# Zero matmuls in TensorE's early gaps, and a new planned order, in a fused decay-attention and feed-forward kernel

## The chip, the cores and the metric

The kernel runs on one core of a Trainium2 chip. The metric is the device time of one launch in microseconds; the median over several runs is compared. The core has five engines with their own instruction queues: TensorE (PE) for matmuls, VectorE (DVE), ScalarE (ACT), GpSimd (POOL), and SyncE (SP), which here issues all DMAs. TensorE writes its results to PSUM, and in this kernel only VectorE and ScalarE read them there.

## The reference

Inputs are q, k, v and f_logit, each of shape (4, 8, 768, 48): 4 batches, 8 heads, 768 steps, 48 channels; and two weights, w_in (384 x 2048) and w_out (2048 x 384). All are float32, and so is the output (3072, 384).

```python
f = 1.0 / (1.0 + np.exp(-f_logit))
for t in range(S):
    state = f[:, :, t, :, None] * state + np.einsum('bhd,bhe->bhde', k[:, :, t], v[:, :, t])
    y[:, :, t] = np.einsum('bhd,bhde->bhe', q[:, :, t], state)
x = y.transpose(0, 2, 1, 3).reshape(B * S, H * D)
h = x @ w_in
out = (h * np.cos(h)) @ w_out
```

So the first part is a gated linear attention whose state decays per channel, and the second a feed-forward layer with h cos(h) as its activation.

## The kernel before

**Tiles.** The 768 steps of a batch are cut into six chunks of 128 steps, which gives 24 chunks n = 0 to 23. For each chunk the cumulated log decay is a matmul with a triangular matrix (L505 to L517), two exponentials give b and bi (L522), and q times b and k times bi are the bf16 pair qk (L567, L680). TensorE transposes qk (L587, L698), or from chunk 12 on mostly a DMA does (L689). Then come the scores (L600, L711), their mask (am, L606, L714), the chunk's contribution to the state (L620, L724), which VectorE and GpSimd add and decay into sz (L540, L547), and the output y, already transposed (L653, L744). Its copy is xT (L458). Chunks 0 to 11 are worked on in pairs (DUAL: 0, 2, 4, 6, 8, 10), whose loads hold two consecutive steps per row.

**The feed-forward part** works on 13 units of tokens: two of 128 and eleven of 256 (`UNITS`). For each unit, `h` (L768) multiplies xT by w_in into two banks of PSUM, ScalarE takes the cosine (L775), VectorE the product gT (L778), and `o` (L790) multiplies gT by w_out. ot is the copy that SyncE stores (L799, L802). A unit's `h` is split into parts j, each of which reads its own columns of w_in and depends on no other part. Both weights are loaded in four blocks each (L424), through the buffers of gT, and cast to bf16 by one of three engines (L430).

**Groups.** Four chunks make a group of the decay; its exponentials and logarithm need another table on ScalarE than the cosine, so each group locks that table until it is done. From the second group on, the first `exp` waits for all the group's loads of f, and a "gate" makes it wait for a given number of cosines (`PR["gate"]`).

**What sets the order.** No engine's order follows the loops. `build` lists some 800 operations with a cost for each engine that can take them, the values that they read and write, and a priority from the table `PR`. `Plan.run` then simulates the engines: of the operations that can start on an engine within 120 ns of the earliest one, it takes the one with the lowest priority number, gives it a buffer, and moves that engine's clock on. `PIN` binds single operations, by number, to one engine. The instructions are then emitted in the order of planned starts. So a load is issued when its buffer is free and its priority is the lowest among those left; transfers follow one another on a planned bus. The planner knows of a slow clock of TensorE: a value `hot` rises with busy time and falls with idle time, both with a constant of 2500 ns, and below 0.5 a matmul group costs 1.9 times as much.

**PSUM** has eight banks, held as four tiles of two. `apart` tells the dependency tracking that two operations on different banks of one tile do not conflict.

Of the kernel before, what the change touches and what calls it, by code (L numbers as in the profile page):

```python
# [10 lines left out]
BF16 = mybir.dt.bfloat16  # L11
# [105 lines left out]
class Plan:  # L117
# [4 lines left out]
    FORM = 96.0  # L122
    TABLE = 1290.0
# [34 lines left out]
    def run(self):  # L158
        free = {"PE": 0.0, "ACT": 800.0, "DVE": 3500.0, "POOL": 4500.0, "SP": 750.0}
        table, lock, bus, hot, pe_end, form, sent = None, None, 0.0, 0.0, 0.0, "full", []  # L160
        left = {}
# [7 lines left out]
        order, n = [], len(self.ops)  # L169
        while len(order) < n:  # L170
# [46 lines left out]
            o.cost = cost  # L217
            if e == "PE":
                hot *= math.exp((pe_end - s) / 2500.0)
                if hot < 0.5:  # L220
                    cost *= 1.9
                hot = 1.0 - (1.0 - hot) * math.exp(-cost / 2500.0)
                pe_end, form = s + cost, o.form[1]
            o.start = s
            free[e] = s + cost
            if o.dma is not None:
                bus = max(s + cost + 700.0, bus) + o.dma
                o.end = bus + 1250.0
                sent.append(bus)
                if len(sent) > 3:  # L230
                    free[e] = max(free[e], sent[-4] + 900.0)
            else:
                o.end = s + cost + (self.PE_LAT if e == "PE" else 55.0 if e in ("ACT", "DVE") else 0.0)
                o.lat = o.end - s - cost
# [13 lines left out]
        order.sort(key=lambda o: (o.start, o.seq))  # L248
        self.makespan = max(o.end for o in order)
# [3 lines left out]
def apart(tc, o, base):  # L253
# [13 lines left out]
    if banks and len(others) == len(banks):  # L267
        for b in banks:
# [11 lines left out]
    "at": [1.29, -46.96, -60.77, -65.31, -72.81, -88.9, -62.2, -78.56, -65.41, -84.16, -49.49, 6.81, 12.89,  # L280
          14.83, 48.99, 87.93, 101.11, 142.54, 101.56, 112.3, 125.58, 54.78, 57.75, 54.86],
    "dec": [47.91, 7.43, -56.35, -90.55, -146.08, -64.43],
    "f": [-34.92, 30.83, -12.01, 57.34, 6.81, 46.82, 6.06, 8.26, 16.01, 51.17, 25.08, -28.88, 70.17, 25.27,
          33.52, 29.11, 45.05, 53.82, 30, 41.02, 75.42, 105.25, 101.8, 47.02],
    "h": [18.15, -30.97, -41.55, -0.98, 22.93, -34.89, 0.62, 10.73, 30.17, 30.71, 68.39, 4.86, 95.08],
    "k": [-26.25, -35.58, -7.84, -14.12, 9.23, 20.62, 9.36, 29.64, 15.73, -3.08, 14.9, 28.23, 13.74, 17.17,
          50.2, 52.92, 39.09, 29.41, 58.65, 34.81, 116.3, 77.26, 139.17, 143.04],
    "o": [24.63, -19.31, 41.7, 78.77, 63.07, 110.4, 28.5, 147.24, 133.25, 171.17, 181.78, 182.53, 223.04],
    "tq": [40.18, 24.86, 49.05, 16.89, -14.63, -13.53, -72.99, 30.71, 100.53, 84.21, 40.41, 92.28, 63.29,
          8.72, -34.92, -31.89, -4.13, 9.55, 29.5, 39.68, 64.12, 95.56, 100.49, 121.09],  # L290
    "v": [-13.48, 17.98, -0.36, -1.26, 5.93, -16.14, 10.21, 31.08, 11.8, 9.11, 19.3, 20.54, 41.94, 22.2,
          47.4, 31.46, 38.38, 19.76, 32.92, 47.16, 53.68, 101.87, 117.21, 44.48],
    "w_in": [-6.83, -2.34, 0.21, 1.62],
    "w_out": [4.81, 3.28, 2.34, 8.4],
    "wc": [-90.87, -90.11, -69.83, -52.76, -136.89, -232, -120.5, -196.66],
    "gate": [None, 8, 6, 1, 19, 12],
}
PIN = {1: "POOL", 3: "ACT", 5: "ACT", 9: "DVE", 11: "POOL", 13: "DVE", 34: "POOL", 37: "POOL", 39: "ACT", 43:
       "ACT", 54: "DVE", 55: "DVE", 82: "DVE", 102: "POOL", 103: "POOL", 104: "DVE", 105: "POOL", 107: "DVE",
       111: "DVE", 124: "ACT", 164: "DVE", 165: "POOL", 167: "ACT", 169: "ACT", 182: "DVE", 204: "DVE", 210:  # L300
       "ACT", 222: "DVE", 228: "DVE", 243: "ACT", 244: "ACT", 283: "POOL", 284: "POOL", 286: "DVE", 293: "ACT",
       306: "ACT", 333: "DVE", 346: "POOL", 347: "POOL", 348: "POOL", 349: "POOL", 364: "ACT", 386: "ACT", 415:
       "ACT", 430: "ACT", 451: "DVE", 457: "DVE", 472: "POOL", 481: "ACT", 487: "ACT", 496: "DVE", 517: "DVE",
       523: "ACT", 547: "DVE", 558: "ACT", 579: "DVE", 585: "DVE", 600: "POOL", 608: "DVE", 623: "ACT", 644:
       "DVE", 665: "POOL", 674: "DVE", 680: "ACT", 689: "DVE", 731: "ACT", 740: "DVE", 746: "ACT", 752: "DVE",
       773: "DVE", 779: "ACT"}


def build(nc, cpool, ppool, q, k, v, f_logit, moe_w_in, moe_w_out, out):
# [11 lines left out]
    def tl(shape, dt, name):  # L321
        return cpool.tile(shape, dt, name=name)

    ident = tl([128, 128], BF16, "ident")
# [70 lines left out]
    P.banks = base  # L395
    HB = lambda a, d=D: a.rearrange("p (h d) -> p h d", d=d)
# [36 lines left out]
    def load(t, src, b, c, n, prio, nm, flat=lambda a: a):  # L433

        if n not in DUAL:
            P.op(nm + str(n), {"SP": 430.0}, lambda e: nc.sync.dma_start(
                out=HB(t.ap), in_=src[b, :, c * C:(c + 1) * C, :].rearrange("h p d -> p h d")),
                writes=[t], prio=prio, dma=1050.0)
            return
# [235 lines left out]
    def attend(b, c, n, ld, bt, bi, i, prio):  # L675
# [12 lines left out]
        if n in TURN_QK:  # L688
            P.op("tq", {"SP": 420.0}, lambda e: nc.sync.dma_start_transpose(out=qkt.ap, in_=qk.ap),  # L689
                 reads=[qk], writes=[qkt], prio=PR["tq"][n], dma=1600.0)  # L690
# [64 lines left out]
    def moe(t0, T):  # L755
# [26 lines left out]
        for i in range(T // C):  # L782
            r0, ot, pr = t0 + i * C, Val(otS), PR["o"][UNIT[t0]] + i
            pieces = [(0, d_model)] if r0 + C < n_tokens else [(0, 256), (256, d_model)]
            for a, z in pieces:
# [10 lines left out]
                def store(e, half=half, r0=r0, a=a, z=z):  # L796
# [4 lines left out]
                    else:  # L801
                        nc.sync.dma_start(out=out[r0:r0 + C, a:z], in_=half.ap)  # L802
                P.op("st_o", {"SP": 420.0 if r0 // C // 2 * 2 not in DUAL else 840.0}, store, reads=[half],
                     prio=pr, dma=545.0 * (z - a) / d_model)
# [33 lines left out]
def kernel(  # L838
# [13 lines left out]
    with tc.manual_schedule():  # L852
# [4 lines left out]
        for o in order:  # L857
# [4 lines left out]
            del made[:]  # L862
            o.fn(o.eng)
# [33 lines left out]
```

## Time and profile before

| | |
|---|---|
| median of 5 runs | 191.67 us (190.46 to 192.27) |
| the profiled execution | 192.27 us, its span from first to last instruction 190.5 us |
| TensorE busy | 178.1 us (94%) |
| VectorE, ScalarE, GpSimd busy | 131.1, 125.8, 68.1 us |
| moved by DMA | 33.14 MB, 174 GB/s over the span |

The profile is of one execution. In a row of groups, "x24" is a count; a bracket tells the engine's idle time before the group and what ended it. The 40 slices are of 4.76 us each; a digit is a busy share in tenths. "PEclk" is the clock that the throttle granted. Matmuls are pipelined, so the duration of one matmul is longer than the distance between two; the time of a group over its count is nearer to the cost.

### The profile page before, as it was taken

To read this page: it belongs to the slowest core of one execution; us is meant where nothing else is said; L and a number is where in the kernel's file an instruction comes from. 1 tells how busy PE (TensorE), PEld (TensorE's weight loads), DVE (VectorE), ACT (ScalarE), POOL (GpSimd) and SP (SyncE) were. 2 spreads that over 40 slices of the span, in tenths; PEclk is the share of its full clock that TensorE was granted. 3 is DMA by queue.
4 is the path that set the end of the run, shared out by engine and by line. 5 is a ranking of instruction groups with operands and counts; after the bars stand their busy time and mean duration, and the time that the engine had idled before them with its cause. 6 is when DMAs were issued, how large, how long until landed. Compare 5 with 4: busy or idle time off the path is not lost.

```text
span 190.5 us, 5879 instructions
## 1 busy us (share of the span) xinstructions
PE 178.1 (94%) x2512; PEld 133.2 (70%) x2512; DVE 131.1 (69%) x161; ACT 125.8 (66%) x152; POOL 68.1 (36%) x102
## 2 busy tenths in 40 slices
PE   0689999999979999999999999999999999999993
PEld 0567888766667866678886668866676776788663
DVE  5459797929767967965796195999389399366610
ACT  5683678987357898789789658899663360266511
POOL 8318353009403026885246696025752202000000
PEclk9999999999999999999999999999999999999999
DMA  5999999999999768989999999989710910102022
GB/s 148 269 299 353 383 366 248 293 263 236 259 214 229 160 122 164 217 175 184 180 204 159 194 205 168 196 173 190 169 45 0 111 46 18 68 3 83 0 83 83
DMA packets 94121, 33.14 MB, mean 174 GB/s; under 512 B 87312, under 2 KB 92560, under 8 KB 94096
## 3 DMA queue, kind: packets, MB, share of 16 engines
q1 hardware_dynamic: 94096, 32.78, 76.6%
q8 instruction: 19, 0.31, 0.7%
q14 instruction: 6, 0.05, 0.1%
HBM read 25.17 MB, written 4.72 MB: 157 GB/s over the span
## 4 chain that ended last, share of the span: by engine, by line
PE 81%; DVE 5%; SPq 3%; issue 3%; DMA 2%; ACT 2%; POOL 1%; POOLq 0%; DVEq 0%; ACTq 0%
PE ps L768 33%; PE ps L790 30%; PE ps L653 5%; SPq L444 3%; PE ps L744 3%; DVE qk L567 3%; DMA ld<-in_q_dram 2%; PE ps L711 2%; PE ps L600 2%; PE ps L587 2%; ACT bi L522 1%; PE ps L514 1%; PE ps L620 1%; PE ps L724 1%; ACT b L522 1%
## 5 line engine op out<-in xcount | busy, mean ns | idle before, releaser
L775 ACT ACTIVATE cosh<-ps,halfpi 128x1024 bf16<-128x1024 f32 x48 | 53.4, 1115 | 27.5 <-PE ps L768 26.9
L778 DVE TENSOR_TENSOR gT<-ps,cosh 128x1024 bf16<-128x1024 f32 x48 | 58.3, 1221 | 17.3 <-ACT cosh L775 15.4
L790 PE MATMUL ps<-w_out_bf,gT 128*128 128x384 bf16 (+2 forms) x400 | 69.0, 320 | 0.0
L768 PE MATMUL ps<-xT,w_in_bf 128*128 128x256 bf16 (+1 forms) x624 | 67.2, 268 | 0.0
L768 PEld LDWEIGHTS <-w_in_bf 128*128 128x128 bf16 x624 | 57.7, 100 | 7.7 <-issue 0.2
L790 PEld LDWEIGHTS <-gT 128*128 128x128 bf16 x400 | 36.0, 98 | 21.4
L547 POOL TENSOR_TENSOR sz<-st,b 64x192 bf16<-64x192 f32 x32 | 17.0, 530 | 41.3 <-DVE st L540 39.9
L458 DVE COPY ot<-ps 128x384 f32<-128x384 f32 x14 | 7.7, 552 | 13.8 <-PE ps L790 13.7
L606 DVE TENSOR_TENSOR am<-ps,pmask 128x1024 bf16<-128x1024 f32 x12 | 14.3, 1218 | 2.9 <-PE ps L600 2.9
L680 POOL TENSOR_TENSOR qk<-ld,b 128x384 bf16<-128x384 f32 x12 | 12.0, 1001 | 11.3 <-DMA ld<-in_q_dram 5.4
L714 DVE TENSOR_TENSOR am<-ps,umask 128x1024 bf16<-128x1024 f32 x12 | 14.3, 1215 | 0.4 <-PE ps L711 0.4
L458 ACT COPY ot<-ps 128x384 f32<-128x384 f32 (+2 forms) x11 | 5.0, 454 | 13.4 <-PE ps L790 11.9
L540 DVE TENSOR_TENSOR st<-ps,sz 128x384 f32<-128x384 f32 x16 | 8.8, 550 | 7.3 <-PE ps L724 5.9
L430 POOL CAST vb<-ld 128x384 bf16<-128x384 f32 (+1 forms) x11 | 6.8, 623 | 15.3 <-DMA ld<-in_v_dram 12.0
L680 POOL TENSOR_TENSOR qk<-ld,bi 128x384 bf16<-128x384 f32 x12 | 12.0, 1002 | 0.1
L522 ACT ACTIVATE b<-ps 128x776 f32<-128x776 f32 (+1 forms) x14 | 10.1, 723 | 2.9 <-PE ps L511 2.2
L567 POOL TENSOR_TENSOR qk<-ld,b 128x384 bf16<-128x384 f32 x5 | 6.0, 1201 | 16.5 <-ACT b L522 16.5
L482 ACT ACTIVATE f<-f 128x768 f32<-128x768 f32 (+1 forms) x14 | 10.4, 744 | 1.6 <-DMA f<-in_f_logit_dram 1.6
L458 ACT CAST xT<-ps 128x384 bf16<-128x384 f32 x13 | 6.0, 483 | 8.4 <-PE ps L744 6.3
L494 ACT ACTIVATE sp<-f 128x768 bf16<-128x768 f32 (+1 forms) x14 | 10.5, 752 | 0.4
L587 PE MATMUL ps<-ident,qk 128*128 128x128 bf16 x96 | 8.5, 250 | 1.8 <-DVE qk L567 1.8
L522 ACT ACTIVATE bi<-ps 128x768 f32<-128x768 f32 (+1 forms) x14 | 10.1, 718 | 0.0
(67 smaller groups left out, 175.7 us busy)
## 6 DMA issues: line engine op xcount, KB each, us to landing
f<-in_f_logit_dram SPq DMA_DIRECT2D x16, 192.0 KB, 3.7
ld<-in_k_dram SPq DMA_DIRECT2D x16, 192.0 KB, 4.1
ld<-in_q_dram SPq DMA_DIRECT2D x16, 192.0 KB, 4.1
gT<-in_moe_w_in_dram SPq DMA_DIRECT2D x4, 768.0 KB, 9.1
gT<-in_moe_w_out_dram SPq DMA_DIRECT2D x4, 768.0 KB, 11.4
ld<-in_v_dram SPq DMA_DIRECT2D x6, 384.0 KB, 6.0
out_dram<-ot SPq DMA_DIRECT2D x24, 96.0 KB, 2.6
ld<-in_v_dram SPq DMA_DIRECT2D x12, 192.0 KB, 3.9
```

The lines of the kernel that those rows point to most:

```text
L458: (nc.scalar.copy if e == "ACT" else nc.vector.tensor_copy)(out=o, in_=i_)
L522: nc.scalar.activation(out=out_.ap[:, s, :], in_=pc.ap.rearrange("p (m n) -> p m n", m=w)[:, :, 0:n], func=AF.Exp, scale=sign)
L547: eng().tensor_mul(out=like(S_out.ap, pv())[s, ..., r, :], in0=srcap()[s, ..., r, :], in1=d[..., None].broadcast_to(list(d.shape) + [D]))
L567: P.op("qk", {"POOL": 1150.0, "DVE": 800.0}, lambda e, j=j, i=i, src=src, dec=dec: E(e).tensor_mul(out=parts[j][i].ap.rearrange("p e h d - ...
L587: nc.tensor.transpose(out=o[:, j, :, p, x, :], in_=twin(j, 2 * i + p, x), identity=ident)
L606: P.op("am", {"DVE": dve(1024)}, lambda e, sc=sc, am=am: nc.vector.tensor_mul(out=am.ap.rearrange("p r a n -> p (r a n)").rearrange("p (a ...
L680: P.op("qk", {"POOL": 1020.0}, lambda e, j=j, src=src, dec=dec: E(e).tensor_mul(out=qkv()[:, j, :, 0:D], in0=HB(src.ap), in1=HB(dec.ap[:, ...
L714: P.op("am", {"DVE": dve(1024)}, lambda e: nc.vector.tensor_mul(out=am.ap.rearrange("p r a n -> p (r a) n"), in0=sc.ap.rearrange("p (a n) ...
L768: nc.tensor.matmul(ph.ap[:, g * T:(g + 1) * T], lhsT=w_in_bf[:, f0 // 512, m, f0 % 512:f0 % 512 + 128], rhs=x[:, m, :], start=(g % (G // 2 ...
L775: nc.scalar.activation(out=co.ap, in_=ph.ap, func=AF.Sin, bias=halfpi),
L778: P.op("g", {"DVE": dve(1024)}, lambda e, ph=ph, co=co, gv=gv: nc.vector.tensor_mul(out=gv.ap, in0=ph.ap.rearrange("p (g t) -> p g t", t=T ...
L790: nc.tensor.matmul(po.ap[:, 0:z - a], lhsT=gT.ap[:, j, i * C:(i + 1) * C], rhs=w_out_bf[:, j, a:z], start=(j == 0), stop=(j == KF - 1))
```

## The change

There are four parts.

1. A tile of zeros, 128 x 128 in bf16, is set by VectorE at the start. Where the plan has TensorE idle for over 300 ns, between 1.3 and 22 us of planned time, `run` notes the gap, and ahead of the operation that ends it `keep_warm` issues matmuls of zeros by zeros, 128 columns each, into a bank of PSUM that is free then: as many as fit into the gap less 150 ns at 106 ns each before 3 us, and at 62 ns each after. `hot` counts the gap as busy.
2. The planner's times for transfers are altered: the first two arrive 700 ns after the bus, no longer 1250; a single load costs 1090 (1050), a transpose by DMA 1700 (1600), a store of 128 rows 580 (545).
3. All priorities in `PR` are new, and with them the gates.
4. `PIN` is new.

```diff
+    WARM = 1300.0, 22000.0
...
+            if e == "PE" and self.WARM[0] < s < self.WARM[1] and s - max(pe_end, self.WARM[0]) > 300.0:
+                t0 = max(pe_end, self.WARM[0])
+                b = self.banks
+                idle = [(b["free"][i], i) for i in range(len(b["free"])) if not b["held"][i] and
+                        all(v.pool is None or getattr(v.pool, "base", None) is not b or
+                            not v.slot <= i < v.slot + v.pool.size for v in o.vals)]
+                if idle and min(idle)[0] + 200.0 < t0:
+                    warm.append((o, t0, s - 150.0 - t0, min(idle)[1]))
+                hot = 1.0 - (1.0 - hot) * math.exp((t0 - s + 150.0) / 2500.0)
+                pe_end = s - 150.0
...
-                o.end = bus + 1250.0
+                o.end = bus + (1250.0 if len(sent) > 1 else 700.0)
...
-    "f": [-34.92, 30.83, -12.01, 57.34, 6.81, 46.82, 6.06, 8.26, 16.01, 51.17, 25.08, -28.88, 70.17, 25.27,
-          33.52, 29.11, 45.05, 53.82, 30, 41.02, 75.42, 105.25, 101.8, 47.02],
+    "f": [-38.59, 18.88, -27.55, 66.29, -7.75, 21.5, -7.77, -22.58, -0.5, -3.43, -1.06, -20.16, 24.83, -5.25,
+          0.94, 20.24, 52.37, 12.16, 15.88, 21.77, 32.28, 95.9, 96.58, 53.9],
...
-    "k": [-26.25, -35.58, -7.84, -14.12, 9.23, 20.62, 9.36, 29.64, 15.73, -3.08, 14.9, 28.23, 13.74, 17.17,
-          50.2, 52.92, 39.09, 29.41, 58.65, 34.81, 116.3, 77.26, 139.17, 143.04],
+    "k": [-31.87, -10.47, -18.89, -7.06, 2.16, 35.41, 2.56, 49.38, 29.78, -2.84, 35.88, 47.19, 53.19, 51.24,
+          47.55, 56.53, 57.8, 57.06, 75.2, 65.21, 108.13, 70.12, 133.47, 124.41],
...
-    "v": [-13.48, 17.98, -0.36, -1.26, 5.93, -16.14, 10.21, 31.08, 11.8, 9.11, 19.3, 20.54, 41.94, 22.2,
+    "v": [-28.81, 16.94, -16.82, -6.73, 0.16, -25.16, 2.96, 15.04, 4.66, 2.58, 7.61, 35.42, 46.87, 9.22,
...
-    "w_in": [-6.83, -2.34, 0.21, 1.62],
-    "w_out": [4.81, 3.28, 2.34, 8.4],
+    "w_in": [-11.72, -10.79, -22.28, -17.8],
+    "w_out": [-10.63, -5.4, -2.76, -3.52],
...
-    "gate": [None, 8, 6, 1, 19, 12],
+    "gate": [None, 5, 4, 6, 21, 1],
...
+    zeros = tl([128, 128], BF16, "zeros")
+    if nc is not None:
+        nc.vector.memset(zeros, 0.0)
...
+    def keep_warm(t, length, bank):
+
+        w = base["width"]
+        for _ in range(int(length / (106.0 if t < 3000.0 else 62.0))):
+            nc.tensor.matmul(base["tiles"][bank // 2][:, bank % 2 * w:bank % 2 * w + 128], lhsT=zeros,
+                             rhs=zeros, start=True, stop=True)
+    P.keep_warm = keep_warm
...
-                writes=[t], prio=prio, dma=1050.0)
+                writes=[t], prio=prio, dma=1090.0)
...
-                 reads=[qk], writes=[qkt], prio=PR["tq"][n], dma=1600.0)
+                 reads=[qk], writes=[qkt], prio=PR["tq"][n], dma=1700.0)
...
-                     prio=pr, dma=545.0 * (z - a) / d_model)
+                     prio=pr, dma=580.0 * (z - a) / d_model)
...
+            if o in P.warm:
+                P.keep_warm(*P.warm[o])
+                bank = P.warm[o][2]
```

Only the even entries of "f", "k" and "v" count for the pairs of chunks below 12, since one load serves both.

## Prediction

> **What bounds the kernel now.** I read first the page's busy shares and slices, then TensorE's instructions in order of time up to 60 us, then a table of stretches, the loads and their landings, and the priority tables against the order in which SyncE issued.
>
> Page, busy time and slices of 4.76 us:
>
> ```profile
> PE 178.1 (94%) x2512; PEld 133.2 (70%) x2512; DVE 131.1 (69%) x161; ACT 125.8 (66%) x152; POOL 68.1 (36%) x102
> ...
> PE   0689999999979999999999999999999999999993
> ...
> PEclk9999999999999999999999999999999999999999
> DMA  5999999999999768989999999989710910102022
> ```
>
> TensorE is the bound: 12.4 us idle in 190.5. Nearly all of it lies before 12 us, after the last matmul (187.59 to 190.5), and in one hole in the stretch 40 to 60. The DMA engines are full from 2 to 65 us.
>
> TensorE in order of time (start, us, count; idle before it in brackets):
>
> ```profile
> 4.57 0.48 PE L505 MATMUL ps<-sp,incl 128*128 128x384 bf16 x1 [4.57 <-ACT sp L494]
> ...
> 8.00 1.87 PE L587 MATMUL ps<-ident,qk 128*128 128x128 bf16 x16 [1.58 <-DVE qk L567]
> 10.41 0.82 PE L620 MATMUL ps<-vb,qk 64*128 64x96 bf16 x16 [0.54 <-POOL vb L430]
> ...
> 19.83 2.74 PE L768 MATMUL ps<-xT,w_in_bf 128*128 128x128 bf16 x24
> 22.50 0.78 PE L620 MATMUL ps<-vb,qk 64*128 64x96 bf16 x16
> 23.22 1.51 PE L768 MATMUL ps<-xT,w_in_bf 128*128 128x128 bf16 x24
> ```
>
> The same 24 matmuls take 2.74 us at 19.83 and 1.51 us at 23.22. So TensorE runs at half speed until about 22.5 us, and the row of the granted clock, nines throughout, does not show it.
>
> Two groups of the same order, the second hole, and the step that it delays:
>
> ```profile
> 47.95 1.07 PE L587 MATMUL ps<-ident,qk 128*128 128x128 bf16 x16
> ...
> 53.75 0.52 PE L600 MATMUL ps<-qkt 48*64 48x128 bf16 x22 [1.49 <-issue]
> 54.20 0.51 PE L620 MATMUL ps<-vb,qk 64*128 64x96 bf16 x16
> 54.65 2.79 PE L768 MATMUL ps<-xT,w_in_bf 128*128 128x256 bf16 x24
> ```
>
> Sixteen transposes cost 1.07 us here against 1.87 at 8.00. At 52.26 all work of chunks 0 to 3 is done, and TensorE has nothing in its order that is ready: the attention of chunks 4 and 5 has only just delivered its xT. From 54.65 on its idle time is 0.24 + 0.34 us to the last matmul: after that the kernel is pure TensorE throughput.
>
> **What the Trainium skill says.** "TensorE: Matmul & The Clock Gate", Part 1, "What's actually happening": the array runs at 1.2 GHz until it was busy for a window of about 3.4 us, free-running, then at 2.4 GHz, some 107 against 56 ns for 128 columns. The trace agrees: 2.74 against 1.51 us for 24 is 114 against 63 ns, tails included. Part 4 of the page says that transposes do not count as busy for this gate; the trace fits, 12 to 19 us is nearly all busy (transposes and small tiles) and stays slow. Part 3 there says matmuls run strictly in order, so a filler that is too long delays the real matmul behind it; no run here shows it yet. "DMA: Bandwidth & Descriptors", "Queues, rings and completion order": descriptors of one issuer's ring are consumed in order. Roughly so here: v of chunk 2 was issued at 11.3 and landed at 20.6, behind two weight blocks.
>
> **The change part by part.**
>
> *Zeros tile.* One small memset on VectorE at about 0.8 us; the like one (halfpi) takes 0.06, and VectorE waits until 2.01 for masks anyway. Nothing; 0.06 without that cover.
>
> *Fillers, first gap.* From 1.3 us to 150 ns before the first real matmul (4.57): 3120/106 = 29 matmuls. At the half-speed price they run 3.1 us, from about 0.9 to 4.0 us. TensorE is empty there. Nothing on the path.
>
> *Fillers, later gaps, priced 62 ns.* If the clock has risen, they end on time and cost nothing. If not, each 1.4 us gap runs 0.7 over (114/63 is 1.8). With dense work from 0.9 us, one full window has passed between 4.3 and 7.7 us (estimate from that page). So one gap, the one before 8.0, may run over: 0 to 1.0 us on the transposes. I take 0.3, hidden, since the second half of q for chunks 2 and 3 lands only at 13.9 (issued 9.32, 4.6 to landing). They wait for a PSUM bank that the plan holds for free 0.2 us before; bound 0 to 0.3, taken 0.
>
> *What the faster clock gives before 22.5 us.* Busy so far, from the table of stretches: 15.4 us. At full speed, by the later groups of the same lines: transposes 2 x 0.9, h 1.25, scores 2.43 to 1.14, decay sums 4 x 0.45, L620 0.3, L653 0.6: 7.0 us less. So TensorE did 8.4 us of full-speed work by 22.5.
>
> *The new order of loads.* SyncE issues the ready load with the lowest priority number; the old tables give exactly the order that the profile shows. The new tables give: f0, k0/q0, v0, f2, w_in 2, k2/q2, w_in 3, v2, w_in 0 and 1, w_out 0, f6, f4, w_out 1, 3, 2, then f10 (and f8, if its buffer is free), v4, k4/q4, k6/q6. With the old run's pace (2.1 us for a weight block, about 1.45 for 384 KB): q2 lands at 16.0 in place of 13.9, w_in 2 at 12.6 and w_in 3 at 18.1; all four w_in by 24.7, as before. L768 for units 0 and 1 can start with blocks 2 and 3, their j = 1, so the later arrival of 0 and 1 costs nothing while 2.7 us of that work is open.
> By 22.5 us the new kernel can have done the attention of chunks 0 and 1 (4.4), 3.9 of that of chunks 2 and 3, and 2.7 of L768: 11.0 in place of 8.4. Lead: 2.6 us at most.
>
> *The decay of chunks 4 to 7.* Its gate moves from the eighth to the fifth cosine, and f4, f6 land at about 28 to 30, not 33.7 to 34.9. In the old run exp starts at 37.71 and the first b ends at 42.4; q4 had landed at 40.8 (33.0 + 7.8). So now the loads decide: k4/q4 slip behind f10 and perhaps f8, 1.45 us each: q4 at 42.2 to 43.7.
>
> *From q4 to L768 of chunks 4 and 5.* Old: b at 42.4, L768 at 54.65, 12.2 us, with bi, the copies of o and two pairs' products in one VectorE queue. Row by row the necessary part is: qk 1.1, transposes 1.07, copy 1.0, scores 0.57, two masks 2.4, y 0.8, copy 0.55, some 0.8 for handing on: 8.3. I take 9.1, between the two, nearer the lower end as b and bi are long done: L768 at 42.95 + 9.1 = 52.05. That is 2.6 us earlier. Work needed by then: 8.4 + (54.65 - 22.5 - 1.83 idle) = 38.7; available 11.0 + 29.55 = 40.55. It fits with 1.8 us of idle time to spare, so the load chain decides, not the lead.
>
> *PIN, the other priorities, dma constants (1050 to 1090, 1600 to 1700, 545 to 580).* These move casts and copies between ACT, VectorE and GpSimd (66, 69 and 36% busy) and change only the planned order. After 54.65 there is 0.58 us to gain; a worse order costs idle time that the trace can't show. Bounds -0.5 and +2; taken 0. The tail stays 2.9.
>
> Sum: -2.6. Against the profiled execution: span 190.5 and 1.77 around it make its 192.27, giving 189.7. It is the slowest of five; median 191.67, so I predict **189.1**.
>
> **The rivals.**
> *No net gain.* The early work is done sooner, but TensorE then waits longer for chunks 4 and 5: with f10 alone ahead and a chain of 11 to 12 us, L768 starts at 53.2 to 54.4. For it: the full DMA row; chunks 4 and 5 are what was missing at 52. Against: ACT's b, not the load, came last before. 191.0 (190.2 to 191.9).
> *Zeros do not raise the clock* (the gate might see no activity in them). L768 then still warms it at about 20 to 22, and fillers run 1.8 times too long: 7 us of idle time up to 22.5 would be overfilled by up to 5; the loads hide most. 191.5 to 194, say 192.3. For it: nothing in this profile; against: the page speaks of busy, not data.
> *Slower: prefetch ahead of need.* SyncE puts f10 and f8, loads for chunks 8 to 11, before v4, k4, q4. Place: the queue between 36 and 43.7 us. Price: 2.9 us. It decides when q4 lands after 42.4 and the chain keeps its 12.2: 43.7 + 12.2 = 55.9, 1.3 later than before, so 193.0 (192 to 194.5 with more such holes in later groups). If the chain shrinks to 9.1, it decides only after 45.5.
>
> **How the numbers follow.** Forecast 0.52 (own range 187.9 to 190.3: chain 8 to 10.3 us, no or one more load ahead), lead kept in full and all holes closed (187.0 to 187.9) 0.06, no gain 0.17, no warm clock 0.07, prefetch 0.18. The range 187.0 to 193.0 leaves out half of the last case, part of the fourth and little else. About 1% (189.75 and 193.6) is what a measurement of this kernel can tell from none. Faster by that: 0.44 of the forecast's 0.52 and the 0.06: 0.50. Slower: 0.10 of prefetch, 0.02 of the cold clock, and 0.03 for bad pins: 0.15. Within: 0.35.
>
> **What would show it.** Right: about 29 fillers before 4.6 us; sixteen transposes in about 1.0 us at 8; L768 at half speed nowhere; first L768 reads blocks 2 and 3; exp of chunks 4 to 7 near 30; L768 of chunks 4 and 5 near 52. Wrong: 2.7 us for 24 matmuls still at 20; idle time of over 2 us between 43 and 55; new idle time after 60, where I counted none.

## The result: no change, and the profile after

The changed kernel takes 191.78 us (median, 189.85 to 195.14); the kernel before, timed beside it, 191.4. The ratio is 1.0007, 95% interval 0.999 to 1.0024. The 2.6 us of the forecast are not there; the predicted time 189.1 lies 1.4% below. Medians here are over all executions, while a ratio leaves out those of each kernel that took over 1.5% longer than its fastest, so it need not be the quotient of two medians.

The profiled execution of the changed kernel took 191.04 us, its span is 189.3, and its granted clock 0.991. It lies 0.7 us below its median and the profiled execution of before 0.9 above its own. So the 1.2 us by which the two profiles differ can't be put down to the change; they are read here for places, not for the sum.

The page of the changed kernel: busy time, three rows of the slices of 4.73 us, and the group of the fillers (busy us, mean ns; idle time before):

```profile
PE 179.8 (95%) x2606; PEld 135.9 (72%) x2606; DVE 131.0 (69%) x165; ACT 123.3 (65%) x150; POOL 65.2 (34%) x101
...
PE   7968959999999999999999999999999999999993
...
PEclk9996999999999999999999999999999999999999
DMA  5999999998999998988999998899380100021122
...
L417 PE MATMUL ps<-zeros 128*128 128x128 bf16 x94 | 8.3, 253 | 1.0 <-DVE halfpi L346 1.0
```

TensorE looks busier, 179.8 in place of 178.1 us, but 8.3 of that multiplies zeros. By subtraction the real work takes some 171.4 us, 6.7 less than before: most of the early matmuls do run at full speed. The span did not follow, so TensorE without its fillers is idle for some 17.9 us, where it was idle for 12.4. In TensorE's row a 6 stands in the slice from 9.5 us and a 5 in the one from 23.7; in the row of the granted clock a 6 stands in the slice from 14.2, just behind the first of them.

TensorE of the changed kernel in order of time (start, us, what, count; in brackets the idle time ahead of it and what ended it). Lines have moved by 24: L611 are the transposes of q and k, L677 the products with the state and with the masked scores, L792 the products with w_in of the feed-forward layer, L417 the fillers:

```profile
0.99 3.28 PE L417 MATMUL ps<-zeros 128*128 128x128 bf16 x29 [0.99 <-DVE halfpi L346]
4.54 0.48 PE L529 MATMUL ps<-sp,incl 128*128 128x384 bf16 x1 [0.28 <-ACT sp L518]
...
6.12 1.72 PE L417 MATMUL ps<-zeros 128*128 128x128 bf16 x28
7.68 0.61 PE L611 MATMUL ps<-ident,qk 128*128 128x128 bf16 x8
...
12.69 0.23 PE L677 MATMUL ps<-qkt,sz 128*32 128x128 bf16 x1
14.98 0.28 PE L677 MATMUL ps<-qkt,sz 128*32 128x128 bf16 x5 [2.06 <-DVE sz L571]
...
18.09 1.95 PE L792 MATMUL ps<-xT,w_in_bf 128*128 128x128 bf16 x24
...
20.76 0.73 PE L417 MATMUL ps<-zeros 128*128 128x128 bf16 x10
21.33 1.50 PE L792 MATMUL ps<-xT,w_in_bf 128*128 128x128 bf16 x24
...
25.14 0.40 PE L677 MATMUL ps<-qkt,sz 128*32 128x128 bf16 x12 [1.51 <-DVE am L630]
...
28.51 7.26 PE L792 MATMUL ps<-xT,w_in_bf 128*128 128x128 bf16 x80 [0.76 <-issue]
...
55.61 4.10 PE L792 MATMUL ps<-xT,w_in_bf 128*128 128x256 bf16 x36
```

Eight transposes at 7.68 take 0.61 us, where sixteen took 1.87. But three waits have come: 2.06 us for sz at 12.9, 1.51 for a mask at 23.6, and 0.76 of "issue", where TensorE waits for nothing that the profile shows. And 24 matmuls of L792 take 1.95 us at 18.09 against 1.50 at 21.33: the clock was lost again. Ten fillers at 20.76 run while those 24 could have.

The same stretches as a table, TensorE alone (window, length, busy and count, granted clock, DMA share, GB/s):

```profile
12.70:15.00 2.30, 0.24 (x5) 1.00 1.15 258
15.00:18.80 3.80, 3.80 (x95) 0.58 1.04 330
18.80:23.60 4.80, 4.80 (x110) 0.98 1.02 360
23.60:28.50 4.90, 2.65 (x108) 1.00 1.15 317
```

A stretch with 0.24 us of work in 2.30 is followed by one at clock 0.58. The trace's own record has the clock up at 5.36 us, at half from 15.60 to 19.01, and up from there. The DMA engines are full in all four.

VectorE in the same execution shows what the first wait is:

```profile
12.30 0.34 DVE L571 TENSOR_TENSOR sz<-ps,b 64x192 bf16<-64x192 f32 x1
...
13.57 0.96 DVE L454 CAST w_in_bf<-gT 128x1536 bf16<-128x1536 f32 x1 [0.93 <-DMA gT<-in_moe_w_in_dram]
...
14.56 0.36 DVE L571 TENSOR_TENSOR sz<-ps,b 64x192 bf16<-64x192 f32 x1
```

The cast of weight block 2 stands in VectorE's queue ahead of the second sz. It waits 0.93 us for its transfer and then takes 0.96, and sz, whose own inputs are there, waits behind it, with TensorE behind sz.

To see where time goes one needs the real work done by a given moment: each real matmul that has started by then, at what its shape takes from one start to the next at full speed in the later groups (62 ns for a transpose, 56 for 128 columns of L792, 28 and 14 for the tiles of L677, and so on), fillers at nothing.

```
us of full-speed work done by      15     22.5   28.5   40     54.65  60     80
before                             4.19   7.93   13.18  24.59  37.12  42.17  61.72
changed                            3.90   8.80   12.19  23.78  37.90  43.10  62.64
```

The lead is 0.9 us at 22.5, and at 28.5 it is 1.0 behind. In between, at 26.69 us, both kernels have done exactly the same 368 real matmuls, shape by shape. TensorE was busy with them for 19.39 us before and for 14.59 after: the 4.8 us that the faster clock saved have all gone into waiting, with fillers or idle. The changed kernel passes the other in the stretch from 40 to 55, where before had its hole of 1.49 us and the changed kernel has none (0.02 us idle from 40 to 55.65).

### The profile page after: what moved, and what is told of

Its sections match the earlier page's. It is cut to its first block, busy times and chain, and to the rows that moved or that the text cites. A ratio compares the mean times of both kernels' runs of the same rounds, so it can differ in the third digit from the quotient of the medians.

```text
span 189.3 us, 6055 instructions
## 1 busy us (share of the span) xinstructions
PE 179.8 (95%) x2606; PEld 135.9 (72%) x2606; DVE 131.0 (69%) x165; ACT 123.3 (65%) x150; POOL 65.2 (34%) x101
## 4 chain that ended last, share of the span: by engine, by line
PE 79%; DMA 9%; SPq 3%; DVE 3%; ACT 2%; issue 1%; POOL 1%; DVEq 0%
PE ps L792 32%; PE ps L814 28%; DMA ld<-in_q_dram 5%; PE ps L677 5%; DMA gT<-in_moe_w_in_dram 4%; SPq L468 3%; PE ps L768 3%; PE ps L611 2%; PE ps L735 2%; PE ps L624 1%; PE ps L748 1%; POOL qk L704 1%; PE ps L644 1%; DVE qk L591 1%; PE ps L529 1%
## 5 line engine op out<-in xcount | busy, mean ns | idle before, releaser
L802 DVE TENSOR_TENSOR gT<-ps,cosh 128x1024 bf16<-128x1024 f32 x48 | 58.4, 1221 | 16.9 <-ACT cosh L799 15.6
L792 PE MATMUL ps<-xT,w_in_bf 128*128 128x256 bf16 (+1 forms) x624 | 68.2, 266 | 0.8 <-issue 0.8
L814 PE MATMUL ps<-w_out_bf,gT 128*128 128x384 bf16 (+2 forms) x400 | 67.1, 320 | 0.0
L792 PEld LDWEIGHTS <-w_in_bf 128*128 128x128 bf16 x624 | 56.2, 99 | 8.7 <-issue 0.9
L814 PEld LDWEIGHTS <-gT 128*128 128x128 bf16 x400 | 37.2, 98 | 21.8
L482 ACT COPY ot<-ps 128x384 f32<-128x384 f32 (+2 forms) x16 | 7.4, 464 | 21.3 <-PE ps L814 21.3
L591 POOL TENSOR_TENSOR qk<-ld,bi 128x384 bf16<-128x384 f32 x8 | 8.6, 1084 | 26.4 <-DMA ld<-in_k_dram 15.1
L704 POOL TENSOR_TENSOR qk<-ld,b 128x384 bf16<-128x384 f32 x12 | 12.0, 1001 | 12.6 <-DMA ld<-in_q_dram 9.6
L704 POOL TENSOR_TENSOR qk<-ld,bi 128x384 bf16<-128x384 f32 x12 | 12.0, 1002 | 0.0
L482 DVE CAST xT<-ps 128x384 bf16<-128x384 f32 x15 | 8.2, 553 | 5.0 <-PE ps L677 3.0
L482 DVE COPY ot<-ps 128x384 f32<-128x384 f32 x9 | 5.0, 550 | 7.6 <-PE ps L814 7.6
L417 PE MATMUL ps<-zeros 128*128 128x128 bf16 x94 | 8.3, 253 | 1.0 <-DVE halfpi L346 1.0
```

Of the source, the lines that this page charges most:

```text
L482: (nc.scalar.copy if e == "ACT" else nc.vector.tensor_copy)(out=o, in_=i_)
L591: P.op("qk", {"POOL": 1150.0, "DVE": 800.0}, lambda e, j=j, i=i, src=src, dec=dec: E(e).tensor_mul(out=parts[j][i].ap.rearrange("p e h d - ...
L704: P.op("qk", {"POOL": 1020.0}, lambda e, j=j, src=src, dec=dec: E(e).tensor_mul(out=qkv()[:, j, :, 0:D], in0=HB(src.ap), in1=HB(dec.ap[:, ...
L792: nc.tensor.matmul(ph.ap[:, g * T:(g + 1) * T], lhsT=w_in_bf[:, f0 // 512, m, f0 % 512:f0 % 512 + 128], rhs=x[:, m, :], start=(g % (G // 2 ...
L802: P.op("g", {"DVE": dve(1024)}, lambda e, ph=ph, co=co, gv=gv: nc.vector.tensor_mul(out=gv.ap, in0=ph.ap.rearrange("p (g t) -> p g t", t=T ...
L814: nc.tensor.matmul(po.ap[:, 0:z - a], lhsT=gT.ap[:, j, i * C:(i + 1) * C], rhs=w_out_bf[:, j, a:z], start=(j == 0), stop=(j == KF - 1))
```

## The experiments

The theory after the result: the early part is set by waits, and fillers only change what TensorE does while it waits. Rivals: the new order itself costs what the fillers gain; the clock that is lost again at 15.6 is what costs; the fillers cost by what they add to the instruction stream.

**Fillers left out, the new order kept (e1_no_fill).**

```diff
-            if o in P.warm:
+            if False:
```

> The changed kernel with its order unchanged and all 94 zero matmuls left out. Theory A (the fillers raise the clock early, and the new order needs it): TensorE stays at half speed until about 20 to 24 us, the 24 matmuls of L792 at 18 to 21 us take 2.7 us, the work done by 23.6 us falls by some 1.0 us or more, and the time is 1 to 2.5 us above the changed kernel, so 0.5 to 1.2% slower than the kernel before. Rival B (the loads set the pace up to 55 us, whatever TensorE does): within 0.4 us of the changed kernel.

190.63 us, ratio 0.9982 (0.9955 to 1.0009). TensorE in order of time:

```profile
18.20 2.77 PE L792 MATMUL ps<-xT,w_in_bf 128*128 128x128 bf16 x24
...
22.03 1.51 PE L792 MATMUL ps<-xT,w_in_bf 128*128 128x128 bf16 x24
...
25.87 0.40 PE L677 MATMUL ps<-qkt,sz 128*32 128x128 bf16 x12 [1.35 <-DVE am L630]
```

The clock is low until 21.5 us here, 24 matmuls take 2.77, and yet the kernel is not slower than with fillers. By 28.5 us it has done 12.30 of work, against 12.19 with fillers. The mask's wait is nearly the same, 1.35 for 1.51: it belongs to the order, not to the clock. No "issue" hole is left.

**Fillers in the order of before (e2_old_fill).** The old order as it was, with 92 fillers in the gaps of its own plan (its L674 and L789 are L677 and L792 of the changed kernel).

```diff
+    WARM = 1300.0, 22000.0
...
+            if o in P.warm:
+                P.keep_warm(*P.warm[o])
```

> The kernel before with its order unchanged, and 92 zero matmuls in the gaps of its own plan. Theory A: clock up at 4.4 to 7.8 us, up to 6 us less TensorE time before 23 us; the h matmuls of units 0 and 1 no longer run at half speed; work done at 23.6 us rises by 1 to 2 us and the time falls by 0.8 to 2 us. Rival B: early work is gained, but it is given back as a wait between 25 and 45 us; within 0.4 us of the kernel before. Rival C (overfilling): fillers delay the real matmuls, slower by 0.5 us or more.

193.57 us, ratio 1.0049 (1.0014 to 1.0084): fillers alone make the kernel slower. The clock rises at 6.36. By 26.7 us 11.96 of work is done, 0.7 more than before; by 28.5 it is 12.30, 0.9 less. What comes between:

```profile
15.98 0.29 PE L674 MATMUL ps<-am,vb 64*32 64x128 bf16 x9 [0.91 <-issue]
...
28.65 7.14 PE L789 MATMUL ps<-xT,w_in_bf 128*128 128x128 bf16 x78 [1.42 <-issue]
```

Both holes are "issue", and the first one lies inside an operation, after part of its matmuls. Before had such a hole too. Its TensorE in order of time, and then its chain of work that ended last:

```profile
51.91 0.35 PE L600 MATMUL ps<-qkt 48*64 48x128 bf16 x10
```

```profile
52.26 1.49 issue
53.75 0.52 PE ps L600 x22
```

The hole at 52.26 that the forecast was built on also cuts one operation in two, ten matmuls before it and 22 after. Nothing that these 22 read was late. The count of matmuls ahead of each such hole of 0.25 us or more, fillers included:

```
kernel          matmuls ahead: hole, us
before          734: 1.49
after           478: 0.76
e2_old_fill     222: 0.91, 478: 1.42
e3_cast_later   478: 0.90
e4_hole_filled  350: 1.60, 478: 0.84
e7_nofill_cast  350: 0.27
e8_tiny94       478: 1.39
e11_wide_q10    476: 0.47
s_tiny94        478: 1.38
s_fill94        478: 1.66
none in e1_no_fill, e6_wide, e9_wide_short, e10_nofill_q10, s_none
```

222, 350, 478, 734: each is 128 k - 34 (the 476 is two short of it; a trace can lack a few records). A matmul is two instructions (its weights, then itself), so the holes are 256 instructions apart. The Trainium skill, "Runtime: NRT & Kernel Launch", section "Instruction fetch mechanics", says that an engine's instructions come in blocks of 16 KiB, 256 instructions, over a DMA queue of their own, and that the cost of crossing from one block to the next is mostly hidden. The first half agrees: the page's row for the instruction queue counts 20 packets and 0.33 MB after the change, 16,384 bytes each, and 19 before, as many whole blocks as TensorE's 5212 and 5024 instructions fill. The second half holds for most block ends, but not for the twelve holes of the table. In the changed kernel a packet of that queue runs from 25.84 to 27.07, and TensorE goes on at 28.51; in before one runs from 51.34 to 52.26, and it goes on at 53.75. Put side by side, packets and block ends in order, all fifteen traces agree: in each of the twelve holes TensorE goes on 1.33 to 1.58 us after the block's packet has ended, and at the other 268 block ends it enters the block 1.37 us or more after that. So these holes are waits for instructions. In the twelve, the packet starts only 2.6 to 4.1 us after TensorE has entered the block before; TensorE gets through that block's 128 matmuls before the next block has come.

**The cast of weight block 2 later in VectorE's queue (e3_cast_later).**

```diff
         order = P.run()
+        late = next(o for o in order if o.seq == 5)
+        order.remove(late)
+        order.insert(next(i for i, o in enumerate(order) if o.seq == 49) + 1, late)
```

> The changed kernel with one VectorE instruction moved: the cast of w_in block 2 now comes after the state update of chunk 0 (sz, st) and no longer before it. Theory A: the hole of 2.06 us at 12.9 us shrinks to about 0.3, the clock isn't dropped at 15 us, work done by 18.8 us rises by about 2.5 us; the time falls by 1 to 2 us against the changed kernel. Rival B (loads): the hole goes, but the same time is waited before 28 us for the mask of chunks 2 and 3 or for w_in blocks 0 and 1; within 0.4 us of the changed kernel.

192.03 us, ratio 1.0029 (0.9995 to 1.0064): not the gain that the theory of the queue expected. TensorE:

```profile
13.61 0.28 PE L677 MATMUL ps<-qkt,sz 128*32 128x128 bf16 x5 [0.16 <-DVE sz L571]
...
16.34 1.03 PE L611 MATMUL ps<-ident,qk 128*128 128x128 bf16 x8 [0.95 <-DVE qk L591]
```

The wait of 2.06 is gone, so its cause is shown. But TensorE then waits 0.95 for q and k of the next chunks, and the clock falls all the same, from 16.25 to 19.67. At 28.5 us the work done is 12.24, as in the changed kernel.

**The hole filled (e4_hole_filled).** Thirty more zero matmuls where the changed kernel waits for sz.

```diff
+        hole = next(o for o in order if o.seq == 52)
+        P.warm[hole] = (13000.0, 30 * 62.0 + 1.0, hole.vals[-1].slot)
```

> The changed kernel with 30 more zero matmuls (1.9 us at full speed) in the hole at 12.9 us, ahead of the y matmuls that wait there for sz. The hole itself stays. Theory A: the clock stays up through 15 to 19 us; L677, L611 and L792 there take about 1.3 us less in all; if the clock's drop is what costs, the time falls by 0.5 to 1.5 us and the runs with a lower mean clock disappear. Rival B: the gain is given back before 28 us; within 0.4 us of the changed kernel. If only the hole costs, this changes nothing and the moved cast does.

194.18 us over all executions, 1.5% above before's 191.4; the ratio is 1.0016 (0.9976 to 1.0057). Of its executions, 16 of 22 have a clock drop, with a median of 194.54; the other six have 191.36. The profiled one took 195.09, so its places count and its sum doesn't. Its stretches, TensorE alone:

```profile
23.60:27.00 3.40, 1.89 (x83) 1.00 1.13 355
27.00:33.90 6.90, 6.06 (x98) 0.51 1.10 297
```

The drop at 15.6 is gone, 24 matmuls of L792 take 1.51 at 17.89. But two waits that end at 22.58 and 26.28 (1.60 of "issue", 1.51 for the mask) bring the drop there, and it then falls on dense work of L792, 6.8 us at half speed. A clock raised early was kept past one thin stretch and lost at the next.

**As many instructions, hardly any time (e8_tiny94).** All fillers of the changed kernel replaced by 94 zero matmuls of two columns ahead of the first real one.

```diff
-        for _ in range(int(length / (106.0 if t < 3000.0 else 62.0))):
-            nc.tensor.matmul(base["tiles"][bank // 2][:, bank % 2 * w:bank % 2 * w + 128], lhsT=zeros,
-                             rhs=zeros, start=True, stop=True)
+        for _ in range(94):
+            nc.tensor.matmul(base["tiles"][bank // 2][:, bank % 2 * w:bank % 2 * w + 2], lhsT=zeros,
+                             rhs=zeros[:, 0:2], start=True, stop=True)
...
+        first = next(o for o in order if o.eng == "PE")
+        P.warm = {first: P.warm[first]}
```

> The changed kernel's order, with its 94 zero matmuls replaced by 94 of 2 columns each, all ahead of the first real matmul: as many instructions as in the changed kernel, hardly any array work. Theory D (TensorE's instructions come in blocks of 256, and where a block ends among small matmuls TensorE waits for the next one): an idle time with no releaser of 0.7 to 1.6 us comes after exactly 222, 350, 478 or 734 matmuls, which the kernel without fillers did not have, and the time is 0.4 to 1.5 us above that kernel's 190.63. If D is wrong, there is no such hole and the time stays within 0.3 us of it. The clock should stay low until 19 us or later, as without fillers.

192.82 us, ratio 1.0052 (1.0023 to 1.008).

```profile
28.93 7.26 PE L792 MATMUL ps<-xT,w_in_bf 128*128 128x128 bf16 x80 [1.39 <-issue]
```

The clock rises at 19.16 only, and the hole is back, after 478 matmuls once more, at the same operation as with real fillers and absent without any. It comes with the number of instructions.

**No fillers and the cast later (e7_nofill_cast).** The edits of e1_no_fill and e3_cast_later together.

```diff
+        order.insert(next(i for i, o in enumerate(order) if o.seq == 49) + 1, late)
...
-            if o in P.warm:
+            if False:
```

> The changed kernel's order without fillers, and the cast of w_in block 2 moved behind the state update of chunk 0. Theory A: 0.91 us of idle time at 15 us goes; since the clock is low there anyway, it can't be dropped; 0.3 to 0.9 us below the 190.63 of the kernel without fillers. Rival B (the mask of chunks 2 and 3, at about 25 us, comes no earlier): within 0.3 us of it.

190.34 us, ratio 0.9932 (0.9907 to 0.9957): some 0.7% faster than before, without a filler. In the profiled execution the clock came up by itself at 15.65 us, ahead of the first dense work, where e1_no_fill has 2.77 us for the same 24 matmuls:

```profile
17.21 1.51 PE L792 MATMUL ps<-xT,w_in_bf 128*128 128x128 bf16 x24
```

By 60 us 45.19 of work is done, against 43.21 in e1_no_fill; by 80 us 63.57 against 62.71. How much of that lead is the moved cast's and how much the clock's isn't separated. Over half of it is given back between, at a wait of 0.99 + 0.23 us for q of chunks 10 and 11 (its lines are shown further down).

**Fewer and wider fillers (e6_wide).** The new order, cast later, and 48 fillers of 128 to 512 columns for the 94.

```diff
...
+        wide = {20: [512] * 4 + [128] * 13, 25: [512] * 2, 38: [512] * 7, 42: [128] * 2, 40: [256] * 2, 93: [256] * 3,
+                106: [512] * 4, 121: [256] * 11}
+        P.warm = {o: (wide[o.seq], P.warm[o][2] if o in P.warm else o.vals[-1].slot) for o in order if o.seq in wide}
```

> The changed kernel's order with 48 zero matmuls in place of 94, most of 256 or 512 columns, which fill the gaps up to 25 us (11 of them in the wait for the mask of chunks 2 and 3, none ahead of L792 at 21 us), and with the cast moved. Theory A with D: the clock comes up at 5 to 8 us and stays up in most runs; no idle time without releaser at 28 us; the mask's wait ends 0.8 to 1.4 us earlier; 189.0 us (188.3 to 189.8), 1.1 to 1.8% below the changed kernel. Rival E (a clock that comes up early is dropped again whatever is done, since the attention's small matmuls don't count as activity): drops in over half of the runs, and 191 to 192.5 us. Rival B: no drop, no hole, and yet within 0.4 us of the kernel without fillers.

190.55 us, ratio 0.9945 (0.992 to 0.9969), on the same chip as e7_nofill_cast: level with it. No execution had a clock drop, and the profile has no block-end hole at 28 us. One filler group failed in its purpose:

```profile
24.23 1.36 PE L417 MATMUL ps<-zeros 128*128 128x256 bf16 x11 [1.50 <-DVE am L630]
```

The eleven that were to run during the mask's wait ran after it, for the PSUM bank that they write was not free before. They took 1.3 us of TensorE.

**Without these eleven (e9_wide_short).** Eleven more of 128 columns stand in the first gap, so the number of instructions stays.

```diff
-        wide = {20: [512] * 4 + [128] * 13, 25: [512] * 2, 38: [512] * 7, 42: [128] * 2, 40: [256] * 2, 93: [256] * 3,
-                106: [512] * 4, 121: [256] * 11}
+        wide = {20: [512] * 1 + [128] * 27, 25: [512] * 2, 38: [512] * 7, 42: [128] * 2, 40: [256] * 2, 93: [256] * 3,
+                106: [512] * 4}
```

> The kernel with 48 wider zero matmuls and the moved cast, but without the 11 in the wait for the mask of chunks 2 and 3, which had begun only when that wait was over; 11 more in the first gap keep the number of instructions. Theory A with D: the 1.36 us of late zero matmuls go; the mask's matmuls start at 24.2 and not at 25.4; TensorE is 1.2 us further ahead at 28.5 us. If that lead lasts, 189.4 us (0.6% below the 190.55 of the version with them). Rival F (a new wait at 77 us, for q of chunks 10 and 11, takes what is over): 190.0 to 190.6, and an idle time of 1 us or more ahead of L611 there. The clock may drop in some runs, since the window at 25 us is less full.

190.48 us, ratio 0.9992 (0.996 to 1.0024), so no gain. The mask's products start at 23.94 and by 28.5 us 14.31 of work is done, 1.6 more than in e6_wide. By 80 us it is 63.33, less than in e7_nofill_cast: the lead went into the wait for q of chunks 10 and 11, here 1.03 + 0.23 us. With the clock up at 5.58 us and not at 15.65, this kernel had done 9.72 of work by 22.5 us, just as much as e7_nofill_cast: ten us of early clock were worth nothing there.

**That load of q earlier (e10_nofill_q10, e11_wide_q10).** In e7_nofill_cast and in e9_wide_short the load of q of chunks 10 and 11 goes ahead of two loads of f in SyncE's order.

```diff
+        early = next(o for o in order if o.seq == 343)
+        order.remove(early)
+        order.insert(next(i for i, o in enumerate(order) if o.seq == 587), early)
```

> The version without zero matmuls and with the moved cast, and in SyncE's order the load of q of chunks 10 and 11 ahead of two loads of f (chunks 18 and 19). Rival F: its wait of 1.2 us in front of L611 at 77.8 to 79.6 us shrinks by 0.6 to 1.2 us, and the time falls from 190.34 by as much, to 189.2 to 189.7. Theory A alone (early lead is kept to the end without this): no change beyond 0.2 us.

> The version with 48 zero matmuls, none of them in the mask's wait, the moved cast, and the load of q of chunks 10 and 11 moved ahead. If both the early lead and the late load count: the fastest of all, 188.6 to 189.4 us, over 1% below the kernel before. If zero matmuls gain nothing over a late clock: equal to the version without them and with the same load order, within 0.3 us.

Without fillers 189.90 us, ratio 0.9939 (0.9911 to 0.9968); with wide ones 190.44, ratio 0.9969 (0.9936 to 1.0002), on the same chip. The wait before the move (e7_nofill_cast), and what is left of it after (e10_nofill_q10):

```profile
78.78 0.62 PE L611 MATMUL ps<-ident,qk 128*128 128x128 bf16 x8 [0.99 <-DVE qk L591]
79.63 0.62 PE L611 MATMUL ps<-ident,qk 128*128 128x128 bf16 x8 [0.23 <-POOL qk L591]
```

```profile
78.47 0.62 PE L611 MATMUL ps<-ident,qk 128*128 128x128 bf16 x8 [0.24 <-POOL qk L591]
```

The work done by 80 us grew from 63.57 to 64.76, so the late load is the cause of that wait. In the time it can't be seen: 0.9932 and 0.9939 lie inside each other's intervals. With wide fillers new waits of 0.75 and 0.57 us came at 94 us. Of two kernels in one order, the one with zero matmuls and few extra instructions has no lead over the one without. But the one without was not slow where it matters: its 24 matmuls of L792 at 17.12 us take 1.51 in this profile.

**One order, three kinds of filler, one chip (s_none, s_tiny94, s_fill94).** The order of e10_nofill_q10 with no fillers, with 94 of two columns first, and with the 94 of the change.

The first leaves the fillers out as e1_no_fill does; the second has the edit of e8_tiny94:

```diff
+        for _ in range(94):
+            nc.tensor.matmul(base["tiles"][bank // 2][:, bank % 2 * w:bank % 2 * w + 2], lhsT=zeros,
+                             rhs=zeros[:, 0:2], start=True, stop=True)
...
+        first = next(o for o in order if o.eng == "PE")
+        P.warm = {first: P.warm[first]}
```

> The changed kernel's order with the cast and the load of q of chunks 10 and 11 moved, no zero matmuls; the control of this set. 189.9 us again (189.4 to 190.4), 0.4 to 0.9% below the kernel before.

> The same order with 94 matmuls of 2 columns ahead of everything. Theory D (blocks of 256 instructions): an idle time without releaser after 350 or 478 matmuls, 0.5 to 1.5 us, and a time 0.5 to 2 us above the control. If instructions cost nothing, within 0.3 us of it.

> The same order with the changed kernel's own 94 zero matmuls in its gaps. If the early clock is worth something, it lies below s_tiny94 by 0.3 to 1 us, and still above the control by 0.2 to 1 us, as the block's end costs what the clock gains. If the clock is worth nothing, it lies level with s_tiny94 or above it; if it is worth more than the blocks cost, below the control.

190.28 us (ratio 0.9932, 0.9902 to 0.9963), 192.01 (1.0043, 1.0015 to 1.0071) and, from six executions only, 193.51 (1.0156, 1.0103 to 1.0208). Instructions that take next to no time cost 1.7 us. The profile of s_tiny94 has a hole of 1.38 us after 478 matmuls and that of s_none has none; that the hole is most of the 1.7 in every execution is not shown. A lost clock is not the reason: executions without a drop have 191.86 against 190.00.

The fillers proper, with the clock up at 5.00 us, are 1.5 us slower still. Not early on: by 60 us s_fill94 has done 43.26 of work, against 43.15 with the small ones, and by 80 us 63.14 against 62.95; by 100 us it is 79.15 against 81.87. The profiled execution of s_none is no measure here: it took 191.73, its clock rose at 19.98, and it was at half again from 26.80 to 30.22, so it has 42.43 by 60 us, where the same program had 45.19 in the profile of e10_nofill_q10. The first line below is where s_fill94's block ends, the second a late wait of its own:

```profile
28.28 7.26 PE L792 MATMUL ps<-xT,w_in_bf 128*128 128x128 bf16 x80 [1.66 <-issue]
...
96.93 0.43 PE L735 MATMUL ps<-qkt 48*128 48x128 bf16 x8 [2.02 <-DMA qkt<-qk]
```

After that second wait the clock was at half from 97.16 to 100.57. Why this transpose came so late in s_fill94 and not in the others is open; the work it loses to s_tiny94 in the profiled execution, 2.7 us, is all lost between 80 and 100 us, and whether that is so in every execution wasn't tried.

**Clock drops, over all executions.** A mean granted clock below 0.995 over the span means at least one stretch at half speed.

```
                 with a drop     median without    median with
before*          12 of 75        191.18            193.64
after            34 of 44        190.83            191.89
e1_no_fill        7 of 22        190.55            191.58
e2_old_fill      10 of 22        192.75            195.19
e3_cast_later    16 of 22        192.56            191.69
e4_hole_filled   16 of 22        191.36            194.54
e8_tiny94         8 of 22        192.60            194.90
e7_nofill_cast    4 of 22        190.27            191.18
e6_wide           0 of 22        190.55            -
e9_wide_short     1 of 14        190.38            190.95
e10_nofill_q10    7 of 22        189.85            190.13
e11_wide_q10      3 of 14        190.20            191.00
s_none            6 of 22        190.00            191.78
s_tiny94          9 of 22        191.86            192.23
s_fill94          4 of 6         193.28            193.87
* as timed beside e1 to e4
```

With the fillers of 128 columns in the new order a drop is the rule; without fillers it is the exception, and with the wide ones it is rarest. In the changed kernel it goes with 1.1 us. In e3_cast_later the executions with a drop are not the longer ones, so what a drop costs depends on where it falls.

## Why the prediction was wrong, step by step

**The bound.** "At 52.26 all work of chunks 0 to 3 is done, and TensorE has nothing in its order that is ready": this step failed. It read "issue" as starvation by the loads. The hole cuts an operation in two and stands at the end of an instruction block, after 734 matmuls, whose packet had ended 1.48 us before TensorE went on. So 1.5 of the 2.6 us that I meant to gain by earlier loads depended on the number of instructions ahead. The hole did go, and others came at 28 us.

**Fillers at nothing.** The first gap went as worked out: 29 from 0.99 to 4.27 us. No gap ran over, as the clock was up by 5.36 (28 fillers in 1.72 at 6.12). But I priced them by their time on TensorE alone. They are 188 instructions more, and each block end comes 94 real matmuls earlier: 1.7 us by s_tiny94 against s_none. I did not look at the instruction queue, which is in the page.

**What the faster clock gives.** 7.0 us less busy time was forecast. For the 368 matmuls done by 26.69 us it is 4.8 less, with up to 1.7 more lost in the 3.41 us at half speed (half of them, an estimate): right in kind, less in size. "By 22.5 us ... 11.0 in place of 8.4" is the step that turned it into a lead, and it failed: by the count above 8.80 in place of 7.93. It counted what TensorE could do, not what was ready. The 2.06 us behind the cast, the drop from 15.60 to 19.01, and ten fillers ahead of ready work took it. The "Lead: 2.6 us at most" was then used at its full size. By 26.69 us nothing of it was left, after the mask's wait; the block end then made it a lag.

**The clock that stays up.** This was no step of its own, and it should have been one. The Trainium skill, "TensorE: Matmul & The Clock Gate", Part 1, gives the gate's window as some 3.4 us, free-running. The record agrees: half speed for 3.41 us in the changed kernel and for 6.83 in e4_hole_filled. What I did not draw from it: a clock raised at 5 us can be taken away at 15.6.

**The loads.** The order read from the tables holds where it is told from the trace: w_in block 2 landed at 13.55 (forecast 12.6), q4 at 41.36 (42.2 to 43.7). The f loads that SyncE puts ahead of later loads stood before q6, not before q4. That takes the slower rival, prefetch ahead of need, its place: q4 was earlier than its point of 42.4.

**The decay of chunks 4 to 7.** "exp ... near 30" failed: it starts at 38.23, against 37.71 before. Loads and the gate both came earlier, and it made no difference; ScalarE's own order decides, which is argued from the trace and not tried. b ends at 42.3, as before.

**From q4 to L768 of chunks 4 and 5.** Forecast 52.05, measured 55.61, later than before. It cost nothing, for TensorE had other work: from 40 to 55.65 it was idle for 0.02 us, as decay sums of chunks 8 to 11 ran in it. The rival "no net gain" gave 190.2 to 191.9 and has the time, but not the place: TensorE did not wait longer for chunks 4 and 5. "Zeros do not raise the clock" fell at 5.36 us.

**The other priorities.** Taken as 0 within -0.5 and +2. e1_no_fill bounds the whole new order, without fillers, to -0.45 to +0.1%, less than half of a per cent either way; with the cast in a better place (e7_nofill_cast, another chip) it is 0.7% faster than before. So the place of that cast is likely a part of the new order which cost, by about half a per cent; the intervals of the two runs (0.9955 to 1.0009, 0.9907 to 0.9957) just touch, and no chip ran both.

**The sum.** New order without fillers: 190.63, ratio 0.9982. With them: 191.78, ratio 1.0007. The two intervals overlap, so in this order the fillers took between nothing and about 1 us: what the clock gained went into waits, and instructions and drops cost. Clear of noise is the set on one chip, in the order with the two moves: 3.2 us from no fillers to all 94, 1.7 of them for the instructions. The fastest kernel of the study has the new order, no fillers, and the two moves: 0.9939 and, on another chip, 0.9932, both intervals below 1.

## What to carry to other kernels

Before you fill an engine's gaps, ask whether what follows is held by that engine or by what it waits for: a faster clock in a stretch that waits for loads and a VectorE queue only lengthens the waits. Find out too when the clock comes up without help; here that could be before the first dense work. Price a filler by its instructions as well as by its time, and take an "issue" hole that cuts an operation in two as a matter of the instruction stream: count the instructions ahead of it in two kernels, and look for the instruction packet that ends ahead of it, before you call it starvation. A clock raised early has to be kept, so look for the next thin stretch, and for what stands behind it.

## What the runs showed of the hardware

- Matmuls of zeros raise the granted clock: at 5.36 us, with 29 of them from 0.99 us on; in all records of kernels with fillers of 128 columns or more at 5.0 to 6.9 us, where one is kept.
- Without them it came up at 14.8 us (s_tiny94), 15.65 (e7_nofill_cast), 19.16 (e8_tiny94), 19.98 (s_none), 21.5 (e1_no_fill) and 23.1 (before). In e7_nofill_cast the attention's own small matmuls raised it: the first group of L792 starts at 17.21.
- Waits among small tiles can lose the clock again: 2.06 us at 12.9 in the changed kernel, 0.95 at 15.4 in e3_cast_later, 1.60 and 1.51 at 21 and 24.8 in e4_hole_filled. They need not: the wait of 1.51 us at 23.6 in the changed kernel lost nothing. It is lost for 3.41 us or twice that.
- TensorE enters a new block of 256 instructions no earlier than 1.33 us after the packet with that block has ended, in 280 block ends of fifteen traces. In twelve of them it stood waiting for it, up to 1.66 us, all within the first 54 us, where the DMA engines are full (share 0.9 and more in the slice). Whether the full DMA engines make the packet late is not shown.
- The row of the granted clock shows 1.00 until the first event on record: in before it holds 1.00 from the start to 23.1 us, where 24 matmuls take 2.74 us and not 1.51. Durations of equal groups tell it, the row doesn't.
